# Two V tiles of one step of a two-layer decode kernel, loaded into the upper 64 partitions through GpSimd's DMA queue

## The chip, the cores and the metric

The kernel runs on one core of one Trainium2 chip. The time is that of the device in microseconds (us), and it is the median of several runs; lower is better. Beside it there is one profiled execution with its trace.

## The reference

Two equal layers, each an attention block over a cached K and V and a gated feed-forward block, for a batch of 4 with one new position. Cut to what matters:

```python
def attention(x, k_cache, v_cache, wq, wo):      # x 4 x 1 x 512
    q = heads(x @ wq)                            # 32 heads of 128
    k, v = repeat(k_cache, 4), repeat(v_cache, 4)  # 8 groups, 4096 positions, 128 wide
    p = softmax(q k^T * 128 ** -0.5)
    return (p v) @ wo
def feed_forward(x, w1, w3, w2):                 # 512 -> 1792 -> 512
    return (silu(x @ w1) * (x @ w3)) @ w2
x = x + attention(layernorm(x), ...); x = x + feed_forward(layernorm(x), ...)
x = x + attention(layernorm(x), ...); x = x + feed_forward(layernorm(x), ...)
```

All is float32. K and V are the same in both layers, 67 MB each, and don't fit the core's memory, so both layers read them from HBM.

## The kernel before, in words

*Steps.* Each layer goes over 8 groups g of heads; layer 0 from 0 to 7, layer 1 from 7 to 0. A group has two steps c, each with half of the positions for all four batch rows: 2048 positions of K (4 MB) and of V (4 MB). So a layer has 16 steps, and layer 1 takes them as (7,1), (7,0), (6,0), (6,1), ... (1,0), (1,1), (0,0), (0,1). K or V of a step is 128 partitions wide and has 8 tiles of U = 1024 columns (512 KB).

*A step's work.* `score` (L351 to L364) multiplies q with the eight K tiles, 4 batch rows by 512 positions. `maximum` and `exponent` (L370 to L377) make p, 128 partitions by 512 positions. `turn` (L379 to L385) transposes p in four matmuls of 128 x 128 into PSUM and VectorE copies it to `pT`, positions on partitions. `weigh` (L403 to L410) multiplies `pT` with the eight V tiles: tile r has positions of quarter r // 2 and the batch rows 2 (r % 2) and 2 (r % 2) + 1, four heads' weights by 512 columns of four blocks. `finish` (L413 to L427) calls `turn` and `weigh`, always one step behind `score`: `score` of step n is issued, then `finish` of step n - 1. The second step of a group also joins the two halves' maxima and sums. `project_o` and `project_q` (L437, L329) are the projections of a group. After 16 steps the feed-forward block follows (L451 to L523), whose last weights, w2, come in seven pieces (`W2_PARTS`).

*Loads.* All loads but that of x go out from SyncE's queue in one fixed order, `plan` (L120 to L187): for each step i of a layer, K of step i, then V of step i - 1. `cache` (L132) puts one in, whole (`TILES` tiles) or in parts. The space is one SBUF tile of 216 blocks of 256 columns. `take` (L94) gives the first hole that is long enough, within `limit`; `give` (L109) frees; `pump` (L192) issues from the plan in order as long as there is room for the next entry, and stops at the first that has none. `done` (L231) is called after the last use of each tile in the program; when all tiles of a load are done, its blocks are free and `pump` goes on. So a load of 32 blocks waits for a K or V load to be used up. In layer 1 the holes lie in blocks 28 to 215, and freed blocks of weights (`vacate`) are added as the layer goes on. A load waits on the chip for the last reader of its blocks; nothing else orders it.

*Other DMAs.* x is loaded from ScalarE's queue. GpSimd issues no DMA; it makes the identity matrix at the start and takes one power (L324) for each layer norm.

Of the kernel before, what the change touches and what calls it, by code (L numbers as in the profile page):

```python
# [8 lines left out]
F32 = mybir.dt.float32  # L9
# [4 lines left out]
B, D, HQ, HKV, SK, DH, F = 4, 512, 32, 8, 4096, 128, 1792  # L14
LAYERS = 2
REP = HQ // HKV
P = 128
# [5 lines left out]
BLOCK = 512  # L23
SC = NB * BLOCK
STEPS = SK // SC
NT = BLOCK // P
ROW = NB * REP
# [3 lines left out]
U = 2 * BLOCK  # L31
TILES = 8
# [8 lines left out]
KB = 256  # L41
# [12 lines left out]

W2_PARTS = ((0, 2), (2, 6), (6, 8), (8, 10), (10, 12), (12, 13), (13, 14))
BUSY = (5, 3, 5, 3, 3, 4, 3, 2)
SCRATCH = 64

# [3 lines left out]
def tile_decode_layers(ctx: ExitStack, tc: tile.TileContext, x, kt, v, wqo, wo0, w1, w3, w2, out):  # L64
    nc = tc.nc
    ctx.enter_context(tc.manual_schedule())
    const = ctx.enter_context(tc.tile_pool(name="const", bufs=1))
    work = ctx.enter_context(tc.tile_pool(name="work", bufs=2))
    psum = ctx.enter_context(tc.tile_pool(name="psum", bufs=1, space=bass.MemoryType.PSUM))
# [4 lines left out]
    def at_wq(g):  # L74
        return PAIRS + 2 * HOME * (HKV - 1 - g)
# [4 lines left out]
    def place(at, n):  # L80
        return space[:, at * KB:(at + n) * KB]
# [12 lines left out]
    def take(n, low=0):  # L94
        for i, (at, size) in enumerate(free):
            a, b = max(at, low, limit[0]), min(at + size, limit[1])
            if b - a >= n:
                free[i:i + 1] = [(c, d - c) for c, d in ((at, a), (a + n, at + size)) if d > c]
                return a
        return None  # L100
# [19 lines left out]
    plan = []  # L120

    def stream(keys, src, low=0):
        plan.append((keys, src, low))


    def keep(at, n, src, given=None):
        plan.append((None, src, (at, n, (at, n) if given is None else given)))
# [4 lines left out]
    def cache(which, layer, g, c, parts, r=0, low=0):  # L132
        src = (kt if which == "k" else v)[g, c]
        for n in parts:
            stream([(which, layer, g, c, r + i) for i in range(n)], src[:, r * U:(r + n) * U], low)
            r += n
# [7 lines left out]
    def w1_load():  # L144
        for k in (0, 2):
            keep(k * F // KB, 2 * F // KB, w1[:, k * F:(k + 2) * F])

    n = len(orders[0])
    parts = {("v", 0, n - 3): (4, 4), ("k", 0, n - 2): (2, 5, 1),
             ("v", 0, n - 2): (2, 2, 2, 2), ("k", 0, n - 1): (1, 2, 1, 4), ("v", 0, n - 1): (2, 2, 2, 1, 1),  # L150
             ("v", 1, 1): (2, 2, 2, 2), ("k", 1, 2): (2, 2, 2, 2), ("k", 1, 3): (4, 4), ("k", 1, 4): (4, 4),
             ("k", 1, 5): (4, 4), ("v", 1, 2): (4, 4), ("v", 1, 3): (4, 4), ("v", 1, 4): (4, 4),
             ("v", 1, n - 2): (4, 4), ("k", 1, n - 1): (4, 4), ("v", 1, n - 1): (4, 2, 1, 1)}
# [3 lines left out]
    for layer in range(LAYERS):  # L157
        steps = orders[layer]
        if layer == 0:
            keep(at_wq(0), HOME, wqo[:, (at_wq(0) - PAIRS) * KB:], (at_wq(0), 0))  # L160
        for i, (g, c) in enumerate(steps):
            if layer and g == TURN:
                if i:
                    cache("k", layer, g, c, (1, 1, 2, 1), 2)
                    cache("v", layer, *steps[0], (1, 1, 1))
                    stream([("k", layer, g, c, 0), ("k", layer, g, c, 1)], None)
                    cache("v", layer, *steps[0], (1, 2, 2), 3)
                continue
            cache("k", layer, g, c, parts.get(("k", layer, i), (TILES,)), low=CORE if layer == 0 and g == TURN else 0)
            if layer == 0 and i in weights:  # L170
                weights[i]()
            if i:
                cache("v", layer, *steps[i - 1], parts.get(("v", layer, i - 1), (TILES,)))
        if layer == 0:
            narrow(CORE, PAIRS)
        cache("v", layer, *steps[-1], parts["v", layer, n - 1])
        if layer == 0:
            w1_load()
            narrow(CORE, SPACE)
        else:  # L180
            stream([("wo", 1)], wo0)
        for u in range(2):
            for k in (0, 2):
                a = 4 * KC * FW[0] * u + 4 * FW[u] * k
                stream([("w3", layer, u, k), ("w3", layer, u, k + 1)], w3[:, a:a + 8 * FW[u]])
        for a, b in W2_PARTS:
            stream([("w2", layer, a)], w2[:, a * D:b * D])  # L187

    state = {"next": 0}
    where, left, room = {}, {}, {}  # L190

    def pump():  # L192
        while state["next"] < len(plan):
            keys, src, dst = plan[state["next"]]
            if keys == "limit":
                limit[:] = dst
            elif keys is None:
                at, n, given = dst
                if given[1] and not claim(*given):
                    return  # L200
                nc.sync.dma_start(place(at, n), src)  # L201
            else:
                width = 2 * U if src is None else src.shape[-1]
                at = take(width // KB, dst)
                if at is None:
                    return
                dst = place(at, width // KB)
                if src is None:
                    for i in range(3):
                        nc.scalar.activation(dst[:, i * BLOCK:(i + 1) * BLOCK], stored[i], AF.Copy)  # L210
                    nc.sync.dma_start(dst[:, 3 * BLOCK:], kt[TURN, STORED, :, 3 * BLOCK:2 * U])
                else:
                    nc.sync.dma_start(dst, src)  # L213
                n = width // len(keys)
                left[state["next"]] = len(keys)
                room[state["next"]] = (at, width // KB)
                for i, key in enumerate(keys):
                    where[key] = (dst[:, i * n:(i + 1) * n], state["next"])
                    if key[0] == "k" and key[2] == TURN and key[1] == 0:
                        for (c, r), m in KEPT.items():  # L220
                            if key[3] == c and r <= key[4] < r + m:
                                where[("k", 1, *key[2:])] = where[key]
                                kept.add(key)
            state["next"] += 1
# [3 lines left out]
    def loaded(*key):  # L228
        return where[key][0]

    def done(*key):  # L231
        if key in kept:
            return
        i = where[key][1]
        left[i] -= 1
        if left[i] == 0:
            give(*room[i])
            pump()
# [10 lines left out]
    ident = const.tile([P, P], F32, name="ident")  # L249
# [19 lines left out]
    qT = const.tile([P, B, 32 + LEAD], F32, name="qT")  # L269
    nc.vector.memset(qT, 0.0)  # L270
    oT = const.tile([P, REP, B], F32, name="oT")
    hT = const.tile([P, 14, B], F32, name="hT")
    sums_ps = psum.tile([P, 2, P], F32, name="sums_ps")
    nc.vector.memset(sums_ps, 0.0)
    x_ps, misc = sums_ps[:, 0, :], sums_ps[:, 1, :]
    o_ps = [psum.tile([P, NB * DH], F32, name=f"o{i}", tag=f"o{i}") for i in range(STEPS)]
# [99 lines left out]
                             accum_out=acc[:, 2 + i:3 + i])  # L376
        return p  # L377

    def turn(p):  # L379
        pt = turned()  # L380
        for n in range(NT):
            nc.tensor.transpose(pt[:, n, :], p[:, n, :], ident)  # L382
        pT = work.tile([P, NT, B, ROW], F32, name="pT", bufs=1)
        nc.vector.tensor_copy(pT, pt.rearrange("p n (b r) -> p n b r", b=B)[:, :, :, 0:ROW])  # L384
        return pT  # L385

    def join_maxima(acc):
# [15 lines left out]
    def weigh(layer, g, c, i, pT):  # L403
        for r in range(TILES):
            t = loaded("v", layer, g, c, r)
            for j in range(2):
                b = 2 * (r % 2) + j
                nc.tensor.matmul(o_ps[i][32 * b:32 * b + ROW, :], pT[:, r // 2, b, :],  # L408
                                 t[:, j * NB * DH:(j + 1) * NB * DH], start=(r < 2), stop=(r >= TILES - 2))
            done("v", layer, g, c, r)  # L410


    def finish(layer, g, c, i, p, acc, after=None):  # L413
        pT = turn(p)
        if i < STEPS - 1:
            p = exponent(*after)
            weigh(layer, g, c, i, pT)
            return p
        join_sums(acc)
        o = work.tile([P, NB * DH], F32, name="o", tag="p", bufs=1)  # L420
        nc.vector.tensor_scalar(o, o_ps[0], acc[:, 12:13], None, op0=ALU.mult)  # L421
        weigh(layer, g, c, i, pT)
        for j in (0, 2):
            s = slice(j * DH, (j + 2) * DH)
            nc.vector.scalar_tensor_tensor(o[:, s], o_ps[1][:, s], acc[:, 13:14], o[:, s], op0=ALU.mult,  # L425
                                           op1=ALU.add)
        return o  # L427
# [99 lines left out]
    for layer in range(LAYERS):  # L527
        xT, rstd, factor = layernorm(x_sb, rowsum)
        steps = orders[layer]
        project_q(layer, steps[0][0], xT, rstd, factor)  # L530
        accs, before = {}, None
        for n, (g, c) in enumerate(steps):
            i = n % STEPS
# [4 lines left out]
            if n == 0:  # L538
                p = exponent(i, ps, accs[g])
            elif i == 0:  # L540
                o = finish(layer, *before, p, accs[before[0]])
                turn_o(o)
                p = exponent(i, ps, accs[g])
            else:
                if n > 1:
                    project_o(layer, steps[n - 2][0], small("rowsum"))
                p = finish(layer, *before, p, accs[g], (i, ps, accs[g]))
# [59 lines left out]
```

## Time and profile before

| | |
|---|---|
| median of 3 runs | 711.67 us (711.61 to 711.69) |
| the profiled execution | 712.09 us |
| its span, first to last instruction | 710.2 us |
| mean granted TensorE clock over the span | 0.817 |
| TensorE matmul busy | 452.9 us, 64% |
| VectorE, ScalarE, GpSimd busy | 106.5, 42.3, 2.9 us |
| DMA traffic | 299.80 MB, mean 422 GB/s |

A profile's page has the busy time of each engine, the span in 40 slices, the DMA queues, the chain of work that ended last, and groups of instructions with what they waited for. PE is TensorE's matmul, PEld its weight load, DVE VectorE, ACT ScalarE, POOL GpSimd, SP SyncE, and SPq an issue on SyncE's queue; L12 is line 12 of the kernel. In a group's line stand the busy time, the mean in ns of one, and after the bar the idle time before them with what ended most of it. A share of DMA is the mean over the 16 DMA engines that carry all queues of the core. An operation of two names, `space<-in_v`, writes the first and reads the second.

### The profile page before, as it was taken

The numbers are of one execution on the slowest core, as the hardware profiler recorded it, in microseconds if no ns is written. First come the engines' busy times: TensorE is split into PE (matmuls) and PEld (weight loads), VectorE is DVE, ScalarE is ACT, GpSimd is POOL, SyncE is SP. The second block draws the span as 40 slices with busy tenths as digits, with TensorE's granted clock in tenths as the row PEclk, the third lists the DMA queues.
The fourth block names the chain that finished last, engine by engine and source line by source line (L and its number), as shares of the span: only waits on it lengthen the run. The fifth ranks groups of instructions, "written<-read, shape, count | busy, mean of one in ns | idle before, by whom it ended". The sixth has DMA issues, their size and how long they took to land.

```text
span 710.2 us, 8882 instructions
## 1 busy us (share of the span) xinstructions
PE 452.9 (64%) x3994; PEld 166.2 (23%) x3994; DVE 106.5 (15%) x372; ACT 42.3 (6%) x101; POOL 2.9 (0%) x10
## 2 busy tenths in 40 slices
PE   4542766367662666675687766576566686666887
PEld 2111222122211222121234211122122222222234
DVE  2011011011110111111211110110111111111121
ACT  0000000000000000010111100000000000000011
POOL 0000000000000000000000000000000000000000
PEclk8687687677976889799999988886888867787799
DMA  9999999999999999999999999999999999999996
GB/s 374 434 436 431 426 435 429 430 433 427 435 430 432 433 427 429 434 418 418 420 419 408 412 426 429 428 433 432 430 435 425 431 437 420 438 426 424 426 417 257
DMA packets 19477, 299.80 MB, mean 422 GB/s; under 512 B 2160, under 2 KB 2416, under 8 KB 6384
## 3 DMA queue, kind: packets, MB, share of 16 engines
q1 hardware_dynamic: 19296, 299.18, 99.1%
q8 instruction: 31, 0.51, 0.3%
q10 hardware_dynamic: 144, 0.07, 0.0%
q14 instruction: 6, 0.05, 0.0%
HBM read 299.17 MB, written 0.07 MB: 421 GB/s over the span
## 4 chain that ended last, share of the span: by engine, by line
DMA 83%; PE 15%; DVE 1%; issue 1%; SPq 0%; ACT 0%; POOL 0%; ACTq 0%
DMA space<-in_v 47%; DMA space<-in_kt 28%; DMA space<-in_w 8%; PE scores L361 6%; PE o L408 6%; PE sums_ps L442 0%; PE scores L291 0%; PE sums_ps L334 0%; ACT p L375 0%; DVE acc L371 0%; SPq L213 0%; PE o L460 0%; SPq L201 0%; PE sums_ps L432 0%; PE sums_ps L504 0%
## 5 line engine op out<-in xcount | busy, mean ns | idle before, releaser
L408 PE MATMUL o<-space,pT 128*16 128x512 f32 x1024 | 170.1, 806 | 128.6 <-DMA space<-in_v 127.0
L361 PE MATMUL scores<-space,qT 128*32 128x512 f32 x1024 | 157.2, 763 | 81.0 <-DMA space<-in_kt 75.0
L408 PEld LDWEIGHTS o<-space,pT 128*16 128x16 f32 x1024 | 32.6, 117 | 235.2 <-issue 141.3
L361 PEld LDWEIGHTS scores<-space,qT 128*32 128x32 f32 x1024 | 41.0, 134 | 173.2 <-issue 140.6
L371 DVE TENSOR_REDUCE acc<-scores 128x1 f32<-128x512 f32 x32 | 22.1, 692 | 231.1 <-PE scores L361 231.1
L375 ACT ACTIVATE p<-scores,acc 128x512 f32<-128x512 f32 x32 | 22.0, 687 | 456.9 <-PE sums_ps L432 297.9
L425 DVE SCALAR_TENSOR_TENSOR o<-o,acc,o 128x256 f32<-128x256 f32 x32 | 14.0, 479 | 129.9 <-PE o L408 129.9
L392 DVE TENSOR_REDUCE acc<-sums_ps 128x1 f32<-128x8 f32 x16 | 2.7, 166 | 142.8 <-PE sums_ps L391 142.8
L432 PE MATMUL sums_ps<-ident,o 128*128 128x16 f32 x128 | 17.0, 265 | 8.6 <-DVE o L425 8.6
L334 PE MATMUL sums_ps<-space,xT 128*32 128x128 f32 x512 | 19.2, 294 | 3.7 <-DVE acc L392 3.6
L432 PEld LDWEIGHTS sums_ps<-ident,o 128*128 128x128 f32 x128 | 15.5, 191 | 25.3 <-DVE o L425 25.1
L382 PE MATMUL turned<-ident,p 128*128 128x128 f32 x128 | 21.0, 286 | 0.0
L442 PE MATMUL sums_ps<-space,oT 128*4 128x128 f32 x512 | 17.7, 280 | 0.0
L382 PEld LDWEIGHTS turned<-ident,p 128*128 128x128 f32 x128 | 13.6, 142 | 16.9 <-issue 16.0
L442 PEld LDWEIGHTS sums_ps<-space,oT 128*4 128x4 f32 x512 | 14.2, 90 | 10.1 <-issue 9.4
L291 PE MATMUL scores<-ident 128*128 128x128 f32 x80 | 14.6, 300 | 1.4 <-POOL ident masks.py:199 1.4
L334 PEld LDWEIGHTS sums_ps<-space,xT 128*32 128x32 f32 x512 | 13.9, 117 | 5.7 <-DVE acc L392 4.9
L398 PE MATMUL sums_ps<-acc,alike 128*128 128x1 f32 x32 | 6.1, 261 | 13.0 <-DVE acc L397 13.0
L384 DVE COPY pT<-turned 128x256 f32<-128x256 f32 x32 | 13.4, 419 | 4.3 <-PE turned L382 4.3
L393 ACT ACTIVATE acc<-acc 128x2 f32<-128x2 f32 x16 | 4.7, 296 | 144.6 <-DVE acc L392 144.6
L421 DVE TENSOR_SCALAR o<-o,acc 128x512 f32<-128x512 f32 x16 | 12.0, 751 | 0.6
L291 PEld LDWEIGHTS scores<-ident 128*128 128x128 f32 x80 | 9.5, 151 | 6.4 <-issue 4.9
(78 smaller groups left out, 141.5 us busy)
## 6 DMA issues: line engine op xcount, KB each, us to landing
space<-in_kt SPq DMA_DIRECT2D x23, 4096.0 KB, 28.3
space<-in_v SPq DMA_DIRECT2D x22, 4096.0 KB, 32.3
space<-in_v SPq DMA_DIRECT2D x11, 2048.0 KB, 22.0
space<-in_kt SPq DMA_DIRECT2D x9, 2048.0 KB, 19.7
space<-in_v SPq DMA_DIRECT2D x14, 1024.0 KB, 19.8
space<-in_wqo SPq DMA_DIRECT2D x3, 4096.0 KB, 42.7
space<-in_kt SPq DMA_DIRECT2D x7, 1024.0 KB, 11.8
space<-in_w SPq DMA_DIRECT2D x6, 1024.0 KB, 17.2
```

The costliest lines, as they stand in the source:

```text
L291: nc.tensor.transpose(pt[:, 0:P], ident, ident)
L334: nc.tensor.matmul(misc[32 * h:32 * h + 32, :], xT[:, 32 * k:32 * k + 32], w[:, k, h * DH:(h + 1) * DH], start=(k == 0), stop=(k == KC - 1))
L361: nc.tensor.matmul(ps[32 * b:32 * b + 32, :], qT[:, b, at:at + 32], t[:, i * BLOCK:(i + 1) * BLOCK], start=(m < 2), stop=(m >= TILES - 2))
L371: nc.vector.tensor_reduce(acc[:, i:i + 1], ps, axis=AX.X, op=ALU.max, negate=True)
L375: nc.scalar.activation(p.rearrange("p n s -> p (n s)"), ps, AF.Exp, bias=acc[:, i:i + 1], accum_out=acc[:, 2 + i:3 + i])
L382: nc.tensor.transpose(pt[:, n, :], p[:, n, :], ident)
L384: nc.vector.tensor_copy(pT, pt.rearrange("p n (b r) -> p n b r", b=B)[:, :, :, 0:ROW])
L408: nc.tensor.matmul(o_ps[i][32 * b:32 * b + ROW, :], pT[:, r // 2, b, :], t[:, j * NB * DH:(j + 1) * NB * DH], start=(r < 2), stop=(r >= TI ...
L421: nc.vector.tensor_scalar(o, o_ps[0], acc[:, 12:13], None, op0=ALU.mult)
L425: nc.vector.scalar_tensor_tensor(o[:, s], o_ps[1][:, s], acc[:, 13:14], o[:, s], op0=ALU.mult, op1=ALU.add)
L432: nc.tensor.matmul(misc[:, 0:B * REP], o[:, j * DH:(j + 1) * DH], own, start=(j == 0), stop=(j == NB - 1))
L442: nc.tensor.matmul(x_ps[32 * k:32 * k + B, :], oT[:, h, :], w[:, h, k * P:(k + 1) * P], start=(h == 0), stop=(h == REP - 1))
```

## The change

Of step (g 1, c 0) of layer 1, the thirteenth of that layer, V is loaded in two ways. The first six of its eight tiles come as before, in one load of 128 partitions (24 blocks). The last two tiles, 128 partitions by 2048 columns, are put into the upper 64 partitions alone, as two layers of 2048 columns (`a`): partition 64 + s holds the rows s and 64 + s. They take 16 blocks. GpSimd issues them, in eight pairs of DMAs: each pair has eight partitions, 4 apart, and in both layers first the columns from 16 on (`LOW`), 2032 of 2048, and then the first 16. The entry stands in the plan three steps ahead (`AHEAD`): with step i - 1 + 3, just before V of step i - 1, that is, after K of (2, 0).

`turn` then makes one more transpose, of the 128 positions that straddle the third and the last quarter of p, so that the first half of the last quarter comes out on partitions 64 to 127 (`pU`); `sums_ps` has a third column in PSUM for it. `weigh` does the last two tiles in eight matmuls over 64 partitions, two per batch row, in place of four over 128. `SCRATCH`, the descriptor space per partition for DMAs that GpSimd issues, goes from 64 to 512 bytes.

```diff
-SCRATCH = 64
+SCRATCH = 512
+UPPER = ((1, 1, 0),)
+AHEAD = 3
+HALF = P // 2
+LOW = 16
...
+            if i and i - 1 + AHEAD < n and (layer, *steps[i - 1 + AHEAD]) in UPPER:
+                at = steps[i - 1 + AHEAD]
+                plan.append(([("v", layer, *at, r) for r in (TILES - 2, TILES - 1)], "upper", at))
             if i:
-                cache("v", layer, *steps[i - 1], parts.get(("v", layer, i - 1), (TILES,)))
+                cache("v", layer, *steps[i - 1], (TILES - 2,) if (layer, *steps[i - 1]) in UPPER
+                      else parts.get(("v", layer, i - 1), (TILES,)))
...
+            elif src == "upper":
+                at = take(4 * U // KB)
+                if at is None:
+                    return
+                to = place(at, 4 * U // KB).rearrange("p (a n) -> p a n", a=2)
+                rows = v[dst][:, (TILES - 2) * U:].rearrange("(a h i r) n -> h r i a n", a=2, h=2, r=4)
+                for h in range(2):
+                    for r in range(4):
+                        p = HALF + 32 * h + r
+                        nc.gpsimd.dma_start(to[p:p + 29:4, :, LOW:], rows[h, r][:, :, LOW:])
+                        nc.gpsimd.dma_start(to[p:p + 29:4, :, 0:LOW], rows[h, r][:, :, 0:LOW])
+                left[state["next"]] = len(keys)
+                room[state["next"]] = (at, 4 * U // KB)
+                for i, key in enumerate(keys):
+                    where[key] = (to[:, :, i * U:(i + 1) * U], state["next"])
...
+    pU = const.tile([P, B, ROW], F32, name="pU")
-    sums_ps = psum.tile([P, 2, P], F32, name="sums_ps")
+    sums_ps = psum.tile([P, 3, P], F32, name="sums_ps")
...
-    def turn(p):
+    def turn(p, upper):
...
+        if upper:
+            low = sums_ps[:, 2, :]
+            at = (NT - 1) * P - HALF
+            nc.tensor.transpose(low, p.rearrange("p n s -> p (n s)")[:, at:at + P], ident)
+            nc.vector.tensor_copy(pU[HALF:P], low[HALF:P].rearrange("p (b r) -> p b r", b=B)[:, :, 0:ROW])
         return pT
...
+            if (layer, g, c) in UPPER and r >= TILES - 2:
+                for a in range(2):
+                    for j in range(2):
+                        b = 2 * (r % 2) + j
+                        nc.tensor.matmul(o_ps[i][32 * b:32 * b + ROW, :],
+                                         pT[HALF:P, NT - 1, b, :] if a else pU[HALF:P, b, :],
+                                         t[HALF:P, a, j * BLOCK:(j + 1) * BLOCK], start=False, stop=(a == 1))
+                done("v", layer, g, c, r)
+                continue
...
-        pT = turn(p)
+        pT = turn(p, (layer, g, c) in UPPER)
```

## The prediction, made before the changed kernel ran

> **What bounds the kernel now.** I read the page first, for its parts 1 to 4 and 6.
>
> ```profile
> span 710.2 us, 8882 instructions
> ...
> DMA  9999999999999999999999999999999999999996
> ...
> q1 hardware_dynamic: 19296, 299.18, 99.1%
> q8 instruction: 31, 0.51, 0.3%
> ...
> q14 instruction: 6, 0.05, 0.0%
> ...
> DMA 83%; PE 15%; DVE 1%; issue 1%; SPq 0%; ACT 0%; POOL 0%; ACTq 0%
> ...
> L408 PE MATMUL o<-space,pT 128*16 128x512 f32 x1024 | 170.1, 806 | 128.6 <-DMA space<-in_v 127.0
> ...
> space<-in_kt SPq DMA_DIRECT2D x23, 4096.0 KB, 28.3
> space<-in_v SPq DMA_DIRECT2D x22, 4096.0 KB, 32.3
> ```
>
> The DMA row is full but for the last slice, and the chain that ended last is 83% DMA. SyncE's queue q1 alone fills 99.1% of 16 engines' time. A matmul on V waits 128.6 us for V in all. So the kernel ends when the bytes are in, and work on the other engines has cover in almost every step. The queue is deep: a load of 4 MB is on its way for 28.3 to 32.3 us, and most of that it stands behind other loads.
>
> Next I asked for the busy times of short stretches. The last two columns are the mean busy share of the 16 DMA engines and GB/s; a packet counts where it starts.
>
> ```profile
> 200.00:300.00 100.00, 59.80 (x478) 20.98 (x474) 12.90 (x43) 4.48 (x12) 0.00 (x0) 0.77 1.00 431
> ...
> 695.00:699.00 4.00, 4.00 (x67) 2.11 (x58) 1.17 (x2) 2.12 (x3) 0.00 (x0) 1.00 1.03 413
> ...
> 700.00:701.00 1.00, 0.97 (x32) 0.56 (x20) 0.40 (x1) 0.00 (x0) 0.00 (x0) 1.00 0.94 369
> ...
> 701.50:702.00 0.50, 0.50 (x9) 0.29 (x10) 0.33 (x3) 0.00 (x0) 0.00 (x0) 1.00 0.57 229
> ...
> 702.50:703.00 0.50, 0.50 (x21) 0.28 (x10) 0.00 (x0) 0.00 (x0) 0.00 (x0) 1.00 0.57 229
> 703.00:703.50 0.50, 0.50 (x10) 0.33 (x14) 0.00 (x0) 0.00 (x0) 0.00 (x0) 1.00 0.48 193
> ...
> 704.00:704.50 0.50, 0.27 (x2) 0.03 (x2) 0.00 (x0) 0.00 (x0) 0.00 (x0) 1.00 0.48 193
> ...
> 705.00:705.50 0.50, 0.50 (x10) 0.20 (x2) 0.00 (x0) 0.00 (x0) 0.00 (x0) 1.00 0.38 147
> 705.50:706.00 0.50, 0.28 (x13) 0.26 (x16) 0.00 (x0) 0.00 (x0) 0.00 (x0) 1.00 0.37 139
> 706.00:706.50 0.50, 0.36 (x17) 0.10 (x5) 0.00 (x0) 0.00 (x0) 0.00 (x0) 1.00 0.12 45
> 706.50:707.00 0.50, 0.40 (x8) 0.11 (x8) 0.00 (x0) 0.00 (x0) 0.00 (x0) 1.00 0.00 0
> ```
>
> This is the row of steps that matters. In the body all 16 engines work, at 431 GB/s, so 26.9 GB/s each. At the end they don't stop together. From 701.5 to 703 the share is 0.57, nine engines of 16; from 703 to 704.5 it is 0.48, eight; then 0.38, six; then 0.12, two; from 706.5 on none. So **seven engines have nothing left at 701.5, an eighth stops at about 703.1, and eight work on until 705 to 707**. All loads of q1 are 128 partitions wide, and q1 gave each engine the same bytes, as far as the equal steps tell. What sets eight of them back? The page's q8, loads of instructions: 0.3% of 16 engines' 710.2 us is 34 us, 1.1 us for each of 31. On eight engines that is 4.3 us each, on sixteen 2.1 us. The distance between the two halves of the staircase, some 4 to 5 us, fits eight. That is an inference, not a row.
>
> The last pieces of the chain, in order of time (start, us, what):
>
> ```profile
> 677.03 19.22 DMA space<-in_w
> ...
> 696.31 10.66 DMA space<-in_w
> ...
> 707.01 0.45 PE sums_ps L504 x8
> ...
> 707.48 0.29 DVE x_sb L523
> ```
>
> The last weight is in at 706.97, the latest engine's time; the seven early ones had their shares of it by 701.5. What follows takes 3.2 us to the span's end, and nothing here touches it. A load is in when its latest engine is done, and that holds for V and K too: **a change that takes bytes from the late eight and gives them to the early eight moves the end**.
>
> **The change, part by part.** *Bytes.* Two of the eight V tiles of step (g 1, c 0) of layer 1 are 1 MB, 64 KB of each engine's stream on q1, 65536 B / 26.9 GB/s = 2.43 us. All 16 engines lose that. The same 1 MB comes back in eight DMAs of eight partitions, each partition with two runs of 8,128 B, if each partition keeps to one engine and eight engines carry all: 128 KB on each. For short packets I take the rate of 695:699, where the weights come in rows of 4 to 8 KB: 413 / 16 = 25.8 GB/s, 5.08 us. So **eight engines gain 2.43 us and eight lose 5.08 - 2.43 = 2.65 us**. The eight small DMAs (64 B runs) and sixteen completions are short packets; no row prices them. From below they cost nothing; from above, if each of the 16 DMAs held an engine a tenth of the 0.33 us that SyncE takes to issue one (fence below), 0.5 us. I take 0.1 us, close to the bytes.
>
> *Which eight* is open. If they are the early ones (case A), the early half ends at 703.1 + 2.65 + 0.1 = 705.85, the late half at 706.97 - 2.43 + 0.1 = 704.6. The end moves from 706.97 to 705.85, 1.1 us earlier. The single engine that stopped at 703.1 sets it; the others of its half stop 1.6 us before.
>
> The Trainium skill has this in "DMA: Bandwidth & Descriptors". Its section "The descriptor swizzle" has partitions 64 to 127 written by engines 8 to 15 when a transfer spans 128 partitions; its section "Why a DMA increments its semaphore by 16 and not by 1" has a GpSimd DMA with eight shares run on eight engines in a row, from a cursor that moves on with each DMA. By the first rule alone the data would be on 8 to 15; by the second they are wherever the cursor stands, and from a cursor at 0 they would be on 0 to 7 with the small DMAs on the others. No run here shows either, and the trace does not name engines.
>
> *Space and issue times.* The tiles take 16 blocks of 256 columns in all 128 partitions for half of them, three steps early, and the V load of the step shrinks from 32 blocks to 24. Going through take, give and pump with that: the 16 blocks come from a hole of 28 blocks free when K of the step (2, 0) is issued. The next load, V of (3, 1), goes out at the same event as before. From K of (2, 1) on the hole is too short, and each load waits for one event more, until K of (1, 1).
>
> ```profile
> 544.67 0.33 SPq L213 DMA_DIRECT2D space<-in_kt  x1
> 554.48 0.33 SPq L213 DMA_DIRECT2D space<-in_v  x1
> 554.92 0.37 SPq L213 DMA_DIRECT2D space<-in_kt  x1
> 562.49 0.33 SPq L213 DMA_DIRECT2D space<-in_v  x1
> 574.86 0.33 SPq L213 DMA_DIRECT2D space<-in_kt  x1
> 584.80 0.33 SPq L213 DMA_DIRECT2D space<-in_v  x1
> 593.12 0.33 SPq L213 DMA_DIRECT2D space<-in_kt  x1
> 605.40 0.33 SPq L213 DMA_DIRECT2D space<-in_v  x1
> ```
>
> Each line is an issue on SyncE's queue. The third moves to 562.49, the fourth to 574.86, the fifth to 584.80, the sixth to 593.12: 7.6, 12.4, 9.9 and 8.3 us later. The cover is what a load stands in the queue: 4 MB at 431 GB/s are 9.7 us, so 28.3 - 9.7 = 18.6 us for K and 32.3 - 9.7 = 22.6 us for V. So this costs nothing; if a stall elsewhere used up the rest, 6 to 11 us, each us more would empty all engines for one. From 605.40 on events and loads are those of before.
>
> *GpSimd, TensorE, VectorE.* The rows for them:
>
> ```profile
> 634.20 0.66 PE L382 MATMUL turned<-ident,p 128*128 128x128 f32 x4
> ...
> 634.89 0.42 DVE L384 COPY pT<-turned 128x256 f32<-128x256 f32 x1 [0.27 <-PE turned L382]
> ...
> 637.77 4.89 PE L408 MATMUL o<-space,pT 128*16 128x512 f32 x28 [2.92 <-DMA space<-in_v]
> ...
> 694.26 0.55 POOL L324 TENSOR_TENSOR rstd<-ve,half 128x1 f32<-128x1 f32 x1 [306.45 <-DVE ve L323]
> ```
>
> GpSimd has nothing to do for 306 us before 694.26. Its 16 issues (0.33 us each if like SyncE's; some us each would do) start near 545 and are needed at the end of V's matmuls, past 637.77: some 90 us of cover. If GpSimd waits for space, only its own next DMAs stand behind; its next operation is the one at 694.26. In that step, TensorE gets one more transpose (0.66 / 4 = 0.17 us) and 8 matmuls in place of 4 (4 x 4.89 / 28 = 0.70 us), VectorE a copy of half L384's size (under 0.42 us). TensorE had waited 2.92 us for that V, so 0.17 + 0.42 lie under the wait; the 0.70 us after it delay by so much the release of buffers whose loads have 18 us of cover. Without cover these are 1.3 us. A larger descriptor scratch and a third PSUM column cost no time.
>
> **Sum.** Against the profiled execution (712.09 us, 1.9 of it around the span): -1.1 us, 711.0. The median of the runs shown, 711.67, is 0.4 below that execution; the forecast is 711.67 - 1.1 = **710.6 us**. Ends for it: -2.4 us if the engine of 703.1 is spared (its half then ends near 701.5 + 2.75 = 704.3, the late half at 704.6), +0.2 us if the short packets cost 0.5 us and rows from GpSimd a fifth more time: 709.3 to 711.9.
>
> **Rivals.** *B, slower: the data ride on the late eight.* Then the latest engine ends at 706.97 + 2.65 + 0.1 = 709.7, every load from then on is in that much later, and the time is 711.67 + 2.75 = **714.4 us**. It decides wholly on which eight engines take the first DMA of a pair; the point from which it costs is 0, since the late eight have no slack at all. Speaking for it: nothing in the trace ties partitions 64 to 127 to the early engines, nor eight rows from GpSimd to a fixed place. If besides such an engine writes where another already writes all the time, its 5.08 us double, at worst 719.5. I take the plain sum, since no row shows such a doubling. The cursor rule above, from 0 and with engines 0 to 7 the late ones, is this case.
>
> *C, all sixteen engines share the rows, or the small DMAs take turns with the data otherwise than in pairs:* the bytes are as even as before, the staircase keeps its shape, and only short packets are added: 0.1 to 0.5 us, **711.9 us**. This is the case in which the change does not do what it says. The same page's "Rules for kernel authors" calls transfers to disjoint partition halves useless because both spray over all 16 engines; by that rule it comes out here, and no run here shows it.
>
> *D, the queue runs dry* after the later issues, near 575 to 600. For it: 12.4 us is more than half of 22.6. Against it: that cover is a median over 22 loads, and the share of DMA between 200 and 300 is 1.00. If it fell short by 2 us, 713.7 in case C's place; I put it inside C and B.
>
> **Chances.** Between A and B the trace gives no ruling; it shows a half that is early and a half that is late, and eight rows go to one of them. A 0.48, B 0.38, C with D 0.14; the little more for A is a judgement: an engine that serves fixed partitions gives every partition of one half to one set, and then one order of a pair cannot go wrong, whereas B needs the cursor or the wrong half. 0.2% is 1.4 us, about what a measurement of this kernel can tell from no change: under 710.2 is faster, over 713.1 slower. Case A at 1.1 us lies just inside: 0.18 of its 0.48 is faster, 0.30 the same. C adds 0.12 to the same and 0.02 to slower; B 0.35 to slower and 0.03 to the same. So 0.18, 0.45, 0.37. The range takes A's lower end without its last tenth, 709.5, and reaches over B's plain sum, 715.0; A's own range is 709.3 to 711.9.
>
> **What would show it.** Right: the staircase shorter, with the late eight ending some 2.4 us earlier against the early ones, last weight in near 705.9; a GpSimd queue of 1 MB with the issues at 545 to 575; SyncE's issues at 562, 575, 585, 593. Wrong by B: more than eight engines idle from 702, the last weight in near 709.7. Wrong by C: shares as now. Wrong by D: a slice of DMA below 9 near 575 to 600. A busy share above eight sixteenths until the end, with the end later, would say that a GpSimd packet costs more than its bytes.

## The result, and the profile after

The changed kernel takes **722.26 us** (median of 5 runs, 721.45 to 724.96) against 711.69 us (711.61 to 711.95) for the kernel before: a ratio of 1.0152, with a 95% interval from 1.014 to 1.0163. A second series of runs of it gave 722.09 us against 711.77, ratio 1.0148 [1.0134, 1.0162]. The forecast was 710.6, with a range up to 715.0.

These lines of the changed kernel's page answer to those shown of before: the span, the GB/s of 40 slices, the queues, the chain, and the waits of the matmuls on V.

```profile
span 723.1 us, 8930 instructions
...
DMA  9999999999999999999999999999999999999993
GB/s 381 434 435 433 431 430 427 424 430 434 434 435 430 429 430 430 421 423 421 423 408 378 416 431 424 430 434 429 425 377 372 378 433 430 431 430 422 423 417 158
...
q1 hardware_dynamic: 19296, 298.13, 97.9%
q0 software_dynamic: 640, 1.05, 0.4%
...
DMA 66%; PE 31%; DVE 1%; issue 1%; SPq 0%; ACT 0%; POOL 0%; POOLq 0%; ACTq 0%
...
L451 PE MATMUL o<-space,pT 128*16 128x512 f32 x1016 | 189.9, 910 | 77.2 <-DMA space<-in_v 74.1
```

The DMA row is as full as before, so no queue runs dry. But slices 30 to 32 of the GB/s row, about 524 to 578 us, stand at 377, 372 and 378 where their neighbours have 425 to 434. (Slice 22, with 378, is as low in this execution alone: it has 408 before, and 402 in the next execution shown.) **The engines are busy all the time and move less.** The new queue q0 has its 1.05 MB in 640 packets.

This execution was granted a mean TensorE clock of 0.603 (0.817 before). Its chain has 31% of PE and it took 724.96 us; the four others, at clocks of 0.808 to 0.826, took 721.45 to 722.32 us. I read the rest from the profile of the second series, at a clock of 0.813 and 721.73 us. Its page:

```profile
span 719.9 us, 8930 instructions
...
GB/s 378 439 431 431 426 431 431 435 432 427 429 431 432 434 428 432 419 427 419 422 415 402 421 429 426 431 435 427 422 367 359 373 435 429 427 431 422 429 414 225
...
DMA 81%; PE 17%; DVE 1%; issue 1%; SPq 0%; ACT 0%; POOL 0%; POOLq 0%; ACTq 0%
```

The dip is the same, and the chain is DMA again. The last piece of that chain (start, us, what):

```profile
706.11 10.51 DMA space<-in_w
```

The last weight is in at 716.62 instead of 706.97, 9.65 us later, and that is the whole difference of the two profiled executions: 721.73 - 712.09 = 9.64 us. Nothing is lost behind the last weight.

Stretches of the kernel before, around the dip (the last two columns are the busy share of the 16 DMA engines and GB/s):

```profile
524.00:560.00 36.00, 22.00 (x191) 8.39 (x195) 5.87 (x20) 1.85 (x5) 0.00 (x0) 0.86 0.99 425
...
580.00:630.00 50.00, 33.46 (x261) 11.32 (x254) 6.97 (x23) 2.63 (x7) 0.00 (x0) 0.77 1.00 430
```

The same of the changed kernel, second series, with one row near its end:

```profile
520.00:524.00 4.00, 4.00 (x28) 0.94 (x24) 0.00 (x0) 0.00 (x0) 0.25 (x1) 0.64 1.02 350
524.00:560.00 36.00, 18.88 (x133) 6.19 (x129) 4.26 (x14) 1.07 (x3) 4.47 (x8) 0.72 1.00 364
560.00:575.00 15.00, 9.25 (x92) 3.13 (x84) 1.71 (x6) 0.78 (x2) 0.00 (x0) 0.76 1.01 371
...
708.00:709.00 1.00, 1.00 (x18) 0.64 (x7) 0.22 (x1) 0.23 (x2) 0.00 (x0) 1.00 0.91 369
```

Against 430 GB/s the three slow rows lose (4 x 80 + 36 x 66 + 15 x 59) / 430 = 8.3 us of the 9.65. The other 1.3 us are not placed by these rows. At 708 the share is still 0.91, where the kernel before had none left from 706.5.

The stretch is that of GpSimd's DMAs. The first two, the ninth and the last of its 16 issues (start, us, and in brackets the idle time and what ended it):

```profile
515.64 0.72 POOL L224 DMA_DIRECT2D space<-in_v  x1 [128.04 <-PE sums_ps L485]
516.36 0.57 POOL L225 DMA_DIRECT2D space<-in_v  x1
...
525.37 0.56 POOL L224 DMA_DIRECT2D space<-in_v  x1 [5.11 <-DMA space<-in_v]
...
548.76 0.56 POOL L225 DMA_DIRECT2D space<-in_v  x1 [1.88 <-DMA space<-in_v]
```

Eight go out at once, and each of the second eight waits for the landing of an earlier one. The first goes at 515.6, not near 545.

The trace also has the time that each packet took. A row of a wide load from SyncE, 32 KB for one partition, nearly always takes 1.21 to 1.23 us on its engine before the change. In the changed kernel (second series), 314 of the 580 such rows that start from 520 to 575 took over 1.3 us, 1.59 us in the mean. The slow ones go with GpSimd's data: of the rows that overlap in time with a row of GpSimd's data 76% took over 1.3 us, of the others 5%. And they are not those of eight engines alone: of the 27 rows that start from 527 to 530, none took less than 1.41 us.

### The profile page after: what moved, and what is told of

Same layout as the page of the kernel before. It is cut to its first block, busy times and chain, and to the rows that moved or that the text cites. A ratio compares the mean times of both kernels' runs of the same rounds, so it can differ in the third digit from the quotient of the medians.

```text
span 723.1 us, 8930 instructions
## 1 busy us (share of the span) xinstructions
PE 548.1 (76%) x4003; PEld 189.4 (26%) x4003; DVE 108.4 (15%) x373; ACT 42.3 (6%) x101; POOL 12.0 (2%) x26
## 3 DMA queue, kind: packets, MB, share of 16 engines
q0 software_dynamic: 640, 1.05, 0.4%
## 4 chain that ended last, share of the span: by engine, by line
DMA 66%; PE 31%; DVE 1%; issue 1%; SPq 0%; ACT 0%; POOL 0%; POOLq 0%; ACTq 0%
DMA space<-in_v 40%; DMA space<-in_kt 22%; PE o L451 12%; PE scores L390 11%; DMA space<-in_w 3%; PE sums_ps L485 1%; PE scores L320 1%; PE o L503 1%; PE sums_ps L547 1%; PE sums_ps L363 1%; PE turned L411 1%; PE o L509 1%; PE sums_ps L475 1%; DVE pT L413 0%; PE o L444 0%
## 5 line engine op out<-in xcount | busy, mean ns | idle before, releaser
L451 PE MATMUL o<-space,pT 128*16 128x512 f32 x1016 | 189.9, 910 | 77.2 <-DMA space<-in_v 74.1
L390 PE MATMUL scores<-space,qT 128*32 128x512 f32 x1024 | 197.3, 939 | 56.3 <-DMA space<-in_kt 47.7
L390 PEld LDWEIGHTS scores<-space,qT 128*32 128x32 f32 x1024 | 45.5, 150 | 171.2 <-issue 142.4
L475 PE MATMUL sums_ps<-ident,o 128*128 128x16 f32 x128 | 22.7, 309 | 8.7 <-DVE o L468 8.7
L475 PEld LDWEIGHTS sums_ps<-ident,o 128*128 128x128 f32 x128 | 21.3, 247 | 28.3 <-DVE o L468 28.3
L363 PE MATMUL sums_ps<-space,xT 128*32 128x128 f32 x512 | 23.7, 340 | 3.6 <-DVE acc L426 3.6
L411 PE MATMUL turned<-ident,p 128*128 128x128 f32 x128 | 26.1, 334 | 0.0
L485 PE MATMUL sums_ps<-space,oT 128*4 128x128 f32 x512 | 24.7, 352 | 0.0
L485 PEld LDWEIGHTS sums_ps<-space,oT 128*4 128x4 f32 x512 | 17.3, 108 | 18.2 <-issue 14.9
L320 PE MATMUL scores<-ident 128*128 128x128 f32 x80 | 17.1, 343 | 1.4 <-POOL ident masks.py:199 1.4
```

What stands on the lines that cost most here:

```text
L320: nc.tensor.transpose(pt[:, 0:P], ident, ident)
L363: nc.tensor.matmul(misc[32 * h:32 * h + 32, :], xT[:, 32 * k:32 * k + 32], w[:, k, h * DH:(h + 1) * DH], start=(k == 0), stop=(k == KC - 1))
L390: nc.tensor.matmul(ps[32 * b:32 * b + 32, :], qT[:, b, at:at + 32], t[:, i * BLOCK:(i + 1) * BLOCK], start=(m < 2), stop=(m >= TILES - 2))
L475: nc.tensor.matmul(misc[:, 0:B * REP], o[:, j * DH:(j + 1) * DH], own, start=(j == 0), stop=(j == NB - 1))
L485: nc.tensor.matmul(x_ps[32 * k:32 * k + B, :], oT[:, h, :], w[:, h, k * P:(k + 1) * P], start=(h == 0), stop=(h == REP - 1))
```

## The experiments

Two theories stood at the start. **Crossing**: for the same bytes it matters whether an engine writes the partitions that it writes in the 128-partition loads; where it writes those of another, the rate falls. Rival **queue**: rows from GpSimd's queue cost more than their bytes, or the moved space and issues do. The trace does not name engines, so which engine carries a DMA is inferred throughout.

### Order and half: a two by two

*Data into the lower 64 partitions, data first (e1).* Of the matmuls and the transpose only the half changes with it.

```diff
-                        p = HALF + 32 * h + r
+                        p = 32 * h + r
...
-            at = (NT - 1) * P - HALF
+            at = NT * P - HALF
```

> The same GpSimd DMAs in the same order, but into the lower 64 partitions. Theory of crossed writes (the eight engines that took the data are the early ones, but the upper partitions are served by the other eight, so both sets stand in each other's way): now the early eight write the partitions that they serve; the body keeps 430 GB/s while the data come in, and the time is that of case A, 710.6 us, at most 711.7. Theory of GpSimd's queue (its packets slow all sixteen engines wherever they write): the rate falls to some 370 GB/s as in the changed kernel, and the time stays near 722 us. Theory of space (three steps of a 16-block hole leave the queue short): 722 us as well.

Measured: 714.17 us (713.9 to 714.28), ratio 1.0033 [1.0021, 1.0045], kernel before 711.77. Its stretches:

```profile
524.00:560.00 36.00, 23.67 (x179) 8.18 (x179) 5.76 (x19) 1.74 (x5) 4.48 (x8) 0.72 1.01 430
...
704.00:705.00 1.00, 0.91 (x32) 0.75 (x32) 0.00 (x0) 0.00 (x0) 0.00 (x0) 1.00 0.25 98
...
706.00:707.00 1.00, 0.77 (x20) 0.55 (x18) 0.00 (x0) 0.00 (x0) 0.00 (x0) 1.00 0.13 37
707.00:708.00 1.00, 0.82 (x22) 0.37 (x14) 0.00 (x0) 0.00 (x0) 0.00 (x0) 1.00 0.12 47
```

The dip is gone: 430 GB/s with the same 16 issues from GpSimd. But the 710.6 of case A does not come: two engines (a share of 0.12 to 0.13) work on alone, and by the last piece of the chain the last weight is in at 709.06 (start, us, what):

```profile
696.98 12.08 DMA space<-in_w
```

*Upper 64 partitions, small DMA of each pair first (e2).*

```diff
+                        nc.gpsimd.dma_start(to[p:p + 29:4, :, 0:LOW], rows[h, r][:, :, 0:LOW])
                         nc.gpsimd.dma_start(to[p:p + 29:4, :, LOW:], rows[h, r][:, :, LOW:])
-                        nc.gpsimd.dma_start(to[p:p + 29:4, :, 0:LOW], rows[h, r][:, :, 0:LOW])
```

> The changed kernel with the small DMA of each pair first. Theory of crossed writes: the data move to the other eight engines, the late ones, which serve the upper partitions; no rate is lost, but the late eight carry 2.65 us more: 714.4 us (case B), landings of the last weight 2.7 us later than before. Theory of GpSimd's queue: 722 us and 370 GB/s while the data come in. If the order of a pair doesn't choose the engines: 722 us, with the same profile as the changed kernel.

Measured: 714.32 us (714.15 to 714.42), ratio 1.0036 [1.0023, 1.0048]. Its stretches:

```profile
524.00:560.00 36.00, 23.16 (x179) 7.99 (x172) 5.47 (x18) 1.29 (x4) 3.92 (x7) 0.72 1.01 430
...
704.00:705.00 1.00, 1.00 (x31) 0.82 (x33) 0.41 (x3) 0.00 (x0) 0.00 (x0) 1.00 0.40 164
...
707.00:708.00 1.00, 0.82 (x22) 0.36 (x17) 0.00 (x0) 0.00 (x0) 0.00 (x0) 1.00 0.38 147
```

Full rate again, and the last weight is again late, at 709.20, this time with six engines alone. The last piece of the chain:

```profile
698.64 10.56 DMA space<-in_w
```

Two and six make eight, as many as the kernel before has late engines. So the late engines are not one of the two sets of eight: six of them are among those that carry the data in e2, and two among those that carry them in e1.

*The changed kernel again (e3)*, for the same chip and time; its result and profile stand above.

> The changed kernel once more, for a profile at another granted clock (the first had 0.603, other runs of it 0.81). All theories: 721 to 723 us. If the low clock stretched the tail of the first profile, TensorE waits for the last weights again and the span is some 3 us shorter; the loss of DMA rate while the GpSimd data come in is the same 370 GB/s.

Measured: 722.09 us (721.73 to 723.27). The span of the profile is 3.2 us shorter than that at the low clock, and TensorE waits for the last weights again; the dip is the same.

*Lower 64 partitions, small first (e6)*: the edits of e1 and e2 together.

> The data into the lower 64 partitions, with the small DMA of each pair first. Theory of crossed writes: now the engines that serve the upper partitions write the lower ones; both sets stand in each other's way as in the changed kernel, some 365 to 380 GB/s while the data come in, 720 to 724 us. Theory that upper partitions as such are slow: 714 us or less.

Measured: 722.65 us (721.96 to 723.1), ratio 1.0149 [1.0132, 1.0166], kernel before 711.81. Its stretches:

```profile
524.00:560.00 36.00, 17.74 (x133) 5.91 (x125) 4.21 (x14) 1.07 (x3) 3.92 (x7) 0.73 1.01 361
560.00:575.00 15.00, 10.57 (x88) 3.60 (x84) 1.71 (x6) 0.78 (x2) 0.00 (x0) 0.74 0.99 359
```

So:

| | data first | small first |
|---|---|---|
| upper partitions | 722.1 us, 364 GB/s | 714.3 us, 430 GB/s |
| lower partitions | 714.2 us, 430 GB/s | 722.7 us, 361 GB/s |

Neither the order nor the half decides by itself; the pairing does. The Trainium skill, "DMA: Bandwidth & Descriptors", section "The descriptor swizzle", has partitions 0 to 63 written by engines 0 to 7 and 64 to 127 by 8 to 15 in a transfer of 128 partitions, and its section "Why a DMA increments its semaphore by 16 and not by 1" puts eight shares of a GpSimd DMA on eight consecutive engines from a cursor. With a cursor at 0 the data-first order carries on 0 to 7, and then the two slow cells are the crossed ones. No trace here shows the cursor, and the four cells by themselves would fit as well if writing an engine's own partitions were the slow case; the runs e4 and e7 below speak against that.

The time that packets took from 530 to 545 us, by queue (packets, MB, share of 16 engines' time). The changed kernel (e3):

```profile
q1 hardware_dynamic: 179, 5.18, 94.0%
q0 software_dynamic: 179, 0.26, 6.0%
```

The same with the small DMA first (e2):

```profile
q1 hardware_dynamic: 204, 6.03, 93.7%
q0 software_dynamic: 204, 0.26, 4.8%
```

The same 0.26 MB of GpSimd take 6.0% instead of 4.8%, a quarter more. That alone would be little. The loss is in the other line: SyncE's rows take 94.0 / 5.18 = 18.1% per MB instead of 15.5%, 17% more, and they have nearly all of the bytes. In e2, 3 of the 684 rows of 32 KB that start from 520 to 575 took over 1.3 us, against 314 of 580.

### Crossing without GpSimd

*The kernel before, with one V load of 4 MB, that of step (1, 0), issued by SyncE as two loads of 64 partitions (e4).*

```diff
+                elif keys[0][:4] == ("v", 1, 1, 0):
+                    for h in range(2):
+                        nc.sync.dma_start(dst[64 * h:64 * h + 64], src[64 * h:64 * h + 64])
```

> The kernel before, with V of step (1, 0) of layer 1 loaded by SyncE in two loads, the lower and then the upper 64 partitions; no GpSimd DMA. Theory of crossed writes, if a 64-partition load is spread over all sixteen engines: each half is written by sixteen engines through what serves eight, so its 2 MB take as long as 4 MB, 9.7 us in place of 4.9, twice: 9.7 us more, 721.4 us. Theory of GpSimd's queue or of space: no change, 711.7 us.

Measured: 727.83 us (727.73 to 727.93), ratio 1.0226 [1.0212, 1.024]. Its stretches:

```profile
610.00:620.00 10.00, 6.70 (x42) 2.17 (x38) 2.40 (x7) 0.00 (x0) 0.00 (x0) 0.67 1.01 431
620.00:630.00 10.00, 5.47 (x36) 1.72 (x28) 1.05 (x3) 0.78 (x2) 0.00 (x0) 0.67 1.10 269
630.00:640.00 10.00, 5.47 (x28) 1.57 (x32) 0.00 (x0) 0.00 (x0) 0.00 (x0) 0.50 1.00 200
640.00:650.00 10.00, 2.54 (x44) 1.30 (x36) 1.71 (x6) 0.78 (x2) 0.00 (x0) 0.84 0.98 209
650.00:660.00 10.00, 5.76 (x38) 1.57 (x42) 0.17 (x1) 0.11 (x1) 0.00 (x0) 0.62 0.92 367
```

The rate halves, with every engine busy and no DMA from GpSimd. The sign was expected; the size was not: 16.1 us instead of 9.7. Against 431 the four slow rows lose (10 x 162 + 10 x 231 + 10 x 222 + 10 x 64) / 431 = 15.8 us, all but 0.3 of it. The split load has 128 rows of 32 KB, but 206 rows of that size that start from 615 to 660 took over 1.3 us (2.43 us in the mean, 2 of 498 before): whole loads are slowed beside it too. The Trainium skill, "DMA: Bandwidth & Descriptors", section "Rules for kernel authors", says of two transfers to disjoint partition halves that they are not worth it since both run on all 16 engines. This run shows more than that: the same bytes cost 16 us more, with all engines busy.

### Space, issues and GpSimd's queue by themselves

*The changed plan and space, the two tiles loaded by SyncE, 128 partitions wide (e5)*; the extra transpose and the matmuls over 64 partitions are left out.

```diff
-                for h in range(2):
...
+                nc.sync.dma_start(place(at, 2 * U // KB), v[dst][:, (TILES - 2) * U:])
```

> The changed kernel's plan and space (16 blocks held three steps ahead, V of the step in 24 blocks), but the two tiles come through SyncE's queue, 128 partitions wide, and are used as before. Theory of space: 716 us or more, as the later issues leave the queue short. Theory of crossed writes: no cost, 711.7 us, DMA at 430 GB/s between 524 and 560.

Measured: 711.53 us (711.4 to 711.66), ratio 0.9996 [0.9987, 1.0006]. Its issues on SyncE's queue:

```profile
562.14 0.33 SPq L235 DMA_DIRECT2D space<-in_kt  x1
574.67 0.33 SPq L235 DMA_DIRECT2D space<-in_v  x1
585.85 0.33 SPq L235 DMA_DIRECT2D space<-in_kt  x1
595.48 0.33 SPq L235 DMA_DIRECT2D space<-in_v  x1
```

*The same with that one load issued by GpSimd (e7).*

```diff
-                nc.sync.dma_start(place(at, 2 * U // KB), v[dst][:, (TILES - 2) * U:])
+                nc.gpsimd.dma_start(place(at, 2 * U // KB), v[dst][:, (TILES - 2) * U:])
```

> The two tiles through GpSimd's queue in one load of 128 partitions, three steps ahead. Theory of crossed writes: every engine writes the partitions that it serves and all get the same bytes: 711.7 to 712.0 us, and the staircase at the end as before. Theory of GpSimd's queue (already in doubt): clearly over 713 us.

Measured: 711.66 us (711.39 to 711.75), ratio 0.9998 [0.9988, 1.0007]. Its page has the 1.05 MB on GpSimd's queue:

```profile
q1 hardware_dynamic: 19296, 298.13, 98.7%
q0 software_dynamic: 144, 1.05, 0.4%
```

Both intervals hold 1. From 524 to 560 the DMA engines moved 432 GB/s in e5. In e7 GpSimd's load is issued at 475.6, and they moved 436 GB/s from 475 to 500. The space, the late issues and GpSimd's queue cost nothing that can be measured, and the rival falls. These runs also tell which cells of the two by two are the crossed ones. If e7's load is dealt out to the sixteen engines as SyncE's loads are, each engine writes its own partitions there, and that costs nothing; in e4 all engines are busy with a load of one half, so that some must write the other engines' partitions, and that run is the slowest.

### Which of the lower eight are late

*The kernel before, with useless rows of 16 KB from GpSimd into lower partitions (e8, one run)*: seven DMAs of two to eight rows, so that the first two of the eight engines get seven rows each, the next six, and so on down to one, 0.61 us a row (16 KB at 26.9 GB/s). Nothing reads the rows. The second DMA of each pair brings the count to 16.

```diff
+                for n in range(2, 9):
+                    p = 32 * ((n - 1) // 4) + (n - 1) % 4
+                    nc.gpsimd.dma_start(to[p:p + 4 * n - 3:4, :], v[1, 0][0:n, 0:4 * U])
+                    nc.gpsimd.dma_start(junk[0:16 - n, 4 * n:4 * n + 4], v[1, 0][0:16 - n, 0:4])
```

> The kernel before, with dummy loads through GpSimd's queue near 515 us: seven loads of 2, 3, ... 8 rows of 16 KB into lower partitions 4 apart, each followed by a tiny load of 14, 13, ... 8 rows, so that the first data row always falls on the first engine. Engines 0 to 7 get 7, 7, 6, 5, 4, 3, 2, 1 rows of 0.61 us more, engines 8 to 15 nothing. It tells which engines are late by themselves. Theory that all eight early engines are 0 to 7: the engines of the ladder end between 702 and 706, none past 707.2, and the time is within 1 us of before. Theory that two of the late ones are among 0 to 7: two engines end alone past 707, up to 4.3 us later than before by their place on the ladder, and the time is longer by the same.

Measured: 713.14 us beside 711.81. The end of its staircase:

```profile
705.50:706.00 0.50, 0.36 (x16) 0.36 (x16) 0.00 (x0) 0.00 (x0) 0.00 (x0) 1.00 0.37 143
706.00:706.50 0.50, 0.50 (x14) 0.20 (x2) 0.00 (x0) 0.00 (x0) 0.00 (x0) 1.00 0.14 53
706.50:707.00 0.50, 0.32 (x10) 0.19 (x12) 0.00 (x0) 0.00 (x0) 0.00 (x0) 1.00 0.14 53
707.00:707.50 0.50, 0.43 (x16) 0.13 (x8) 0.00 (x0) 0.00 (x0) 0.00 (x0) 1.00 0.07 29
```

The last piece of its chain:

```profile
697.10 10.95 DMA space<-in_w
```

Two engines are alone from 706 and one from 707, and the last weight is in at 708.05, 1.08 us later than before. An early engine with seven rows doesn't explain that: 701.5 + 4.3 = 705.8, and 707.4 even for the one that stopped at 703.1. So a late engine of the lower half got some rows. How many depends on when it ends by itself. As an estimate from e1, that is 709.06 less what the rows cost there (2.75 us by the prediction's sum, 2.23 by the last weight of e2), so 706.3 to 706.8. Then 1.2 to 1.8 us were added, two or three rows. It is one run, and the engines are counted from the order of rows. That two of the lower eight are late agrees with e1; which two is not shown.

## Why the prediction was wrong, point by point

**The bound** was right: DMA has most of the chain in each of these profiles (66% at the low clock, 81% to 86% in the others), and at the clock of before the time moves with the last weight.

**"Which eight is open"** is the step that failed. It asked only whether the carrying engines are early or late, and priced their rows the same either way: 5.08 us on eight engines. There was a second question in the same place, whose partitions these engines write. The prediction named it in case B, "its 5.08 us double, at worst 719.5", and dropped it: "I take the plain sum, since no row shows such a doubling." The doubling was bounded on the carrying engines alone. In the runs the slower packets are above all SyncE's, on more engines than the eight that carry, and the term is not 2.65 us on eight but 8.3 us of lost rate over the whole row. So even "at worst" lay 2.6 us below the 722.1. The four orders and halves show the cost; that the carriers write the other half's partitions is inferred, since no trace names an engine.

**The two rules of the Trainium skill that the prediction cites were enough to ask the second question.** One gives partitions 64 to 127 to engines 8 to 15, the other, from a cursor at 0, gives the data to 0 to 7. The prediction took them as two answers to one question, which of the eights carries. They answer two questions, and together they say that carriers and partitions don't match. What such a mismatch costs is known from the runs alone.

**Case A's end** fails too, without any crossing. "If they are the early ones" supposed that the late eight and one half of 64 partitions could coincide. They don't: six are in one half and two in the other (e1, e2), so that in either half eight rows add their cost to a late engine.

**Case B's price** holds where there is no crossing: 2.75 us were forecast on top of the kernel before, and e2 took 2.55 and e1 2.40 us more than it in the same series (the last weight came 2.23 and 2.09 us later). So the sum of the bytes' rate, the short packets and the cover of the added matmuls, transpose and copy holds, a little on the high side; its parts were not tested one by one. For e1 the agreement is partly luck: case B has the data on the late eight, and here two late engines were enough.

**Space and issues (case D)**: the later issues were worked out as 562.49, 574.86, 584.80 and 593.12; e5 has 562.14, 574.67, 585.85 and 595.48, and costs nothing. **Case C** fell: if 16 engines shared the rows evenly, the two orders couldn't differ by 8 us. The upper end of case A was added up a little low: 703.1 + 5.08 x 1.2 - 2.43 + 0.5 = 707.27 is 0.3 us later than before, not 0.2, which changes nothing here.

**GpSimd's issues** were put "near 545", and start at 515.6. The prediction let them stand behind SyncE's order of the plan. They stand in another queue, and wait only for the last readers of their own blocks and then for their own earlier landings. It cost nothing here, since e1 issues from 517 on too, and so does e2 but for its first small DMA, at 474.0.

**The tells** held one good line: "A busy share above eight sixteenths until the end, with the end later, would say that a GpSimd packet costs more than its bytes." That is what 708 to 709 shows, with a share of 0.91, though most of the excess was on SyncE's packets.

**Open.** Why rows that have nothing to do with GpSimd's slow down beside them, on more than eight engines, was not isolated. That loads of instructions make the eight engines late is still an inference. The trace before speaks for a part of it: the durations of the 31 loads repeat with every eighth load (the first two rounds after the first load: 1069, 1060, 1100, 1100, 1086, 1026, 1026, 1073 ns, then 1068, 1060, 1099, 1100, 1087, 1029, 1028, 1073 ns), as if eight engines took them in turn, some four each. That these are the late eight is not shown. A version that spares the two late engines of the lower half, with rows on the other six alone, was not tried: it needs another layout of p and V. As an estimate from the prediction's terms, six engines would end at 701.5 + 5.08 x 8 / 6 - 2.43 + 0.1 = 705.9, if all of them stopped at 701.5 before. That is 1 us to win, less than the 1.4 us that the prediction puts as the least to be told from none.

## What to carry to other kernels

Before moving bytes between DMA engines, ask two things: which engines carry the new transfer, and which engines write the same partitions in the wide loads beside it. If they are not the same, price the loss for all engines as long as the transfer lasts, not for its own bytes alone; a slice of the profile with a full DMA row and a lower GB/s is its mark. Where the trace doesn't name engines, a run with the other order and a run with the other half tell it. And a staircase at the end is no map: count who is late within each set that can be moved together before giving one set more work.

## What the runs showed of the hardware that was not expected

- 1 MB from GpSimd in rows of 8,128 B, in two of the four pairings of order and half, lowered the rate of the 16 engines from 430 to between 359 and 371 GB/s for some 55 us. In the other two pairings the same 16 DMAs ran at 430.
- In the changed kernel a 32 KB row of SyncE's took 1.59 us in the mean where it was slow (1.21 to 1.23 as a rule before), and slow rows came nearly only while a GpSimd data row was under way.
- A 4 MB load from SyncE split into two halves of 64 partitions ran, with what was beside it, at 200 to 269 GB/s for 30 us, and cost 16.1 us.
- A DMA issue on GpSimd took 0.56 us (0.72 the first), against 0.33 on SyncE's queue. After eight, each waited for an earlier one to land.
